# A new order for the first 620 steps of an mLSTM and two-FFN kernel, with other engines for some of its small operations

## The chip, the cores and the metric

One core of one Trainium2 chip runs the whole kernel. Its engines work side by side, each through a list of its own in order: TensorE (PE) multiplies, VectorE (DVE), ScalarE (ACT) and GpSimd (POOL) do the elementwise work, SyncE (SP) issues the transfers. The metric is the device time of one execution in microseconds; lower is better.

## The reference

Three layers follow one another. B = 4, H = 8, S = 768, D = 40.

```python
# 1. gated linear attention, over t for every batch and head
m_new = max(f[t] + m, i[t])
C = exp(f[t] + m - m_new) * C + exp(i[t] - m_new) * outer(v[t], k[t])
n = exp(f[t] + m - m_new) * n + exp(i[t] - m_new) * k[t]
y[t] = sigmoid(o[t]) * (C @ q[t]) / max(abs(n @ q[t]), 1)
# 2. feed-forward layer on x = y, 3072 rows of 320
h = x @ w_in                          # 320 x 2048
x1 = (max(h, 0) + alpha * min(h, 0)) @ w_out   # 2048 x 320
# 3. eight experts; each row goes to the one with the largest x1 @ w_gate
out = prob * sigmoid(x1 @ w_output_gate[e]) * (max(x1 @ w1[e], 0) @ w2[e])
```

w_in and w_out arrive as 64-bit floats, everything else as 32-bit floats.

## The kernel before

**Precision.** Large products are made of two single-precision numbers in TensorE's fast format: a value is split into a high part (a copy by ACT) and a low part (value minus high part, by DVE or POOL). A product is three partial products. Every split is therefore one ACT instruction and one DVE or POOL instruction.

**Tiling.** Attention works on 24 units u of 128 positions, all eight heads at once; unit u is chunk c = u mod 6 of batch u div 6. The first FFN works on eight blocks n of three units (384 columns), each with 16 slices of 128 hidden features, so that there are 128 pairs k = 16 n + i. The experts follow in slots of 128 rows that were sorted by expert; they lie behind all that the change touches.

**Column tiles.** The product of decayed scores and values (att_b) and that of w_out with the gates' weights (gate_w2) are cut into four products with 32 output partitions each, which run in four column groups of TensorE.

**The order.** Attention, weight decoding, FFN and the expert weights' splitting are cut into steps. `ORDER` is a list of short codes; the n-th time a code appears, its step function is called with its n-th argument. Each step appends its instructions to the engines' lists, and the framework adds the waits. There is no other scheduling: an engine runs its own instructions in the order in which `ORDER` named them, and waits where one is not ready.

```python
with tc.manual_schedule():
    for code in ORDER.split():
        fn, args = steps[code]
        a = next(args)
        fn(*a)
```

The list has 1,616 codes. What they mean:

- `li` / `lo` (load_wi, load_wo; SP, L641) bring one of 16 blocks of w_in / w_out into one of three raw tiles, which the experts' pieces (`el`, L1197) share. `di` / `do` (dec_wi, dec_wo) decode one from 64 to 32 bits in three DVE instructions (L658, L660, L662). `si` / `so` (split_wi, split_wo) split it: ACT at L674 / L691, then DVE or POOL at L675 / L692.
- `gw`, `gc`, `gv`, `gs` carry the gate weights into w_out: transposes (PE, L699), a copy (ACT, L705), products in column tiles (PE, L714), and the split of the result (ACT L720, DVE L721).
- `lq`, `lv`, `lg`, `load_g`, `log` load q and k, k and v, grouped q, decay rows (D) and output gates of attention. `load_gates`, `load_sel`, `load_cst`, `load_wg` and `ga`, `gb`, `gm`, `gates_st`, `ge`, `gt`, `gates_d` make the gates' cumulative decays at the start.
- `ae` (att_e) takes the exponential of the decay rows (ACT, four of L754; POOL's mask, L755); `as` (att_s) makes the scores (PE, L764); `am` (att_m) multiplies the two (DVE, L772); `ab` (att_b) multiplies by the values (PE, L863).
- `pt` (prep_kt) scales the keys (DVE or POOL, L732); `ad` (att_d) makes the state's increment (PE, L817); `au` (att_u) masks it (DVE L837, or ACT in three instructions L835); `av` (att_v) adds it to the decayed state (DVE, L852).
- `ah` (att_h) multiplies q by the state (PE, L786); `an` (att_n) scales that (DVE L807, or ACT in eight instructions L805); `aa` (att_a) adds it to the unit's own part (DVE, L873).
- `ay` (att_y) has five parts: three for the divisor (DVE, L882, L884, L886), the scaling (part 3, "att_r": DVE L894, or ACT in eight instructions L892), and the gating (part 4, "att_y": DVE or POOL, L898, with a copy on POOL, L899). `ac` and `ax` transpose the unit (PE, L910) and split it into the block's x (ACT L920, DVE L921 and L922).
- `F` (ffn1) is the first product of a pair k: eight matmuls of 384 columns (PE, L933) into one of two PSUM banks. `f` (ffn_act) is the leaky ReLU (ACT L946, DVE L948); for k under 24 its result goes to SBUF (v), after that back to PSUM (ph). `g` (ffn_split) splits it (ACT L954, DVE or POOL L955). `S` (ffn2) is the second product: nine matmuls of 336 columns (PE, L967, L968, L970).
- `es` (expert_split) and `et` split a piece of an expert's weights (ACT L1205, DVE or POOL L1206) and store it.

Attention's small products take turns in three PSUM banks, which the step that reads a product gives back.

**The engine of a step.** `OTHER` names, for ten kinds of steps, the indices that do not use the usual engine:

```python
def engine(usual, other, name, i):
    return other if i in OTHER.get(name, ()) else usual
```

Usual engine, and the other one: ffn_split DVE, POOL; prep_kt DVE, POOL; att_y POOL, DVE; expert_split POOL, DVE; att_n, att_r, att_u, att_v DVE, ACT; split_wi and split_wo POOL, DVE.

Of the kernel before, what the change touches and what calls it, by code (L numbers as in the profile page):

```python
# [18 lines left out]
B, H, S, D = 4, 8, 768, 40  # L19
# [97 lines left out]
ae lg lg S g S S F f g ad au av pt ah an ay es F f g ab aa F f ay ay ad au av et ae et S g el load_g el F f es ay  # L117
et F f ay ay ac ax S g es ae S g ah an F f S S et es ay ay et g lv el el bp as am F f F f el g es et pt S S ab aa
ac ax g ad au av F f F f g S g ay lq sg es es S ay lv pt F f ay el lq g F f as am S g F f et es ah an ad au av S
log S g bo F f sg et g load_g load_g ay ay el el F f lg S ae ab aa ay ay ay et S F f S g lq lq S g ae ac ax lg el S  # L120
as am lv load_g load_g load_g es et es et ay ay F f pt F f g g ab aa ae ay ac ax F f S g es ay ay ay ay S F f F f
ae as am lq S g g load_g ah an ad au av ac ax ae el F f lv pt el ae g et ab aa ay ay S es es F f et et g load_g ay
F f S g as am ay ay lv S load_g S F f g F f ah an ab aa ay S el el es ad au av lg ay ae g ay el es F f ac ax g
load_g et et ah an ah an lv es et ae bp ay ay S S S ae as am F f g F f load_g bo g ab aa ae load_g ae F f g S lq el
# [1308 lines left out]
```

## Time and profile before

| | us |
|---|---|
| median of 3 runs | 753.1 |
| lowest and highest run | 750.1 to 753.96 |
| the profiled execution, its own time | 749.58 |
| its span, first to last instruction | 747.7 |
| PE busy | 717.1 (96%) |
| DVE busy | 463.0 (62%) |
| ACT busy | 368.0 (49%) |
| POOL busy | 184.4 (25%) |

The profile is one execution. Its own time has 1.9 us beside the span. Busy time is the time in which an engine had an instruction under way; for PE it includes the overlap of pipelined matmuls. The mean granted clock of TensorE over the span was 0.994 of full speed.

### The profile page before, as it was taken

The numbers are of one execution on the slowest core, as the hardware profiler recorded it, in microseconds if no ns is written. First come the engines' busy times: TensorE is split into PE (matmuls) and PEld (weight loads), VectorE is DVE, ScalarE is ACT, GpSimd is POOL, SyncE is SP. The second block draws the span as 40 slices with busy tenths as digits, with TensorE's granted clock in tenths as the row PEclk, the third lists the DMA queues.
The fourth block names the chain that finished last, engine by engine and source line by source line (L and its number), as shares of the span: only waits on it lengthen the run. The fifth ranks groups of instructions, "written<-read, shape, count | busy, mean of one in ns | idle before, by whom it ended". The sixth has DMA issues, their size and how long they took to land.

```text
span 747.7 us, 18074 instructions
## 1 busy us (share of the span) xinstructions
PE 717.1 (96%) x6347; PEld 672.7 (90%) x6347; DVE 463.0 (62%) x1119; ACT 368.0 (49%) x840; POOL 184.4 (25%) x240
## 2 busy tenths in 40 slices
PE   5879899999999999999999999999999999999997
PEld 4668889999999999999999999998989999999996
DVE  6879997868676676677797877766323322232222
ACT  4747687736656655656755445433323332333322
POOL 2444454413213332100000100022222222232223
PEclk9989999999999999999999999999999999999999
DMA  7977679879797958778888779885957636921000
GB/s 253 289 206 239 193 239 324 271 272 306 259 324 245 285 183 279 237 238 293 262 290 293 240 272 320 303 310 197 422 226 299 261 138 236 425 73 40 31 14 22
DMA packets 81526, 179.56 MB, mean 240 GB/s; under 512 B 8620, under 2 KB 39209, under 8 KB 80156
## 3 DMA queue, kind: packets, MB, share of 16 engines
q1 hardware_dynamic: 77980, 169.66, 66.1%
q0 software_dynamic: 3456, 8.71, 3.5%
q8 instruction: 56, 0.92, 0.5%
q14 instruction: 34, 0.28, 0.1%
HBM read 246.29 MB, written 55.59 MB: 404 GB/s over the span
## 4 chain that ended last, share of the span: by engine, by line
PE 70%; DVE 9%; DMA 5%; ACT 2%; issue 2%; SPq 1%; POOL 0%; POOLq 0%; ACTq 0%; DVEq 0%
PE ph L933 18%; PE p L326 12%; PE po L326 12%; PE acc L967 7%; PE acc L968 6%; PE acc L970 6%; DMA ring<-scr 3%; PE p L424 3%; PE ps L764 2%; DVE ph L948 1%; PE pb L786 1%; PE pd L817 1%; PE xt L386 1%; PE pa L863 1%; DMA kv<-in_kv_dram 1%
## 5 line engine op out<-in xcount | busy, mean ns | idle before, releaser
L933 PE MATMUL ph<-ring 128*128 128x384 f32 x1024 | 199.7, 343 | 2.7 <-DVE ring L955 2.7
L933 PEld LDWEIGHTS ph<-ring 128*128 128x128 f32 x1024 | 178.1, 189 | 7.0 <-DVE ring L955 5.3
L967 PE MATMUL acc<-ring 128*128 128x336 f32 x384 | 122.6, 324 | 0.3 <-ACT ring L954 0.3
L968 PE MATMUL acc<-ring 128*128 128x336 f32 x384 | 119.4, 317 | 0.0
L946 ACT ACTIVATE v<-ph 128x384 f32<-128x384 f32 x128 | 62.6, 490 | 94.1 <-PE ph L933 90.1
L446 DVE TENSOR_SCALAR yo<-po,xg 128x320 f32<-128x320 f32 x26 | 14.3, 551 | 138.3 <-PE po L326 138.3
L326 PE MATMUL po<-ring,hh 128*128 (+1 forms) x432 | 95.6, 308 | 0.0
L948 DVE SCALAR_TENSOR_TENSOR ph<-v,al,ph 128x384 f32<-128x384 f32 x104 | 63.8, 618 | 45.6 <-ACT v L946 45.2
L326 PE MATMUL p<-ring,xh 128*128 (+1 forms) x324 | 89.9, 399 | 0.8 <-DMA ring<-scr 0.8
L970 PE MATMUL acc<-ring 128*128 128x336 f32 x384 | 80.1, 316 | 0.0
L326 PEld LDWEIGHTS po<-ring,hh 128*128 128x128 f32 x432 | 73.2, 187 | 2.3 <-ACT hh L426 0.2
L967 PEld LDWEIGHTS acc<-ring 128*128 128x128 f32 x384 | 72.2, 188 | 1.9 <-ACT ring L954 0.7
L955 DVE TENSOR_TENSOR ring<-ph,ring 128x384 fp32r<-128x384 f32 x104 | 57.4, 555 | 24.9 <-ACT ring L954 22.8
L954 ACT ACTIVATE ring<-ph 128x384 fp32r<-128x384 f32 x104 | 50.6, 489 | 44.1 <-DVE ph L948 40.6
L968 PEld LDWEIGHTS acc<-ring 128*128 128x128 f32 x384 | 72.2, 188 | 0.0
L426 ACT ACTIVATE hh<-p 128x512 fp32r<-128x512 f32 x54 | 29.5, 596 | 86.3 <-PE p L424 86.3
L326 PEld LDWEIGHTS p<-ring,xh 128*128 128x128 f32 x324 | 58.8, 188 | 12.4 <-DMA ring<-scr 1.0
L447 POOL DMA_INDIRECT out_dram<-yo,tok x28 | 28.2, 1005 | 161.5 <-DVE yo L446 130.0
L413 ACT ACTIVATE hr<-p 128x512 f32<-128x512 f32 x56 | 33.6, 600 | 68.3 <-PE p L326 64.7
L326 PE MATMUL po<-ring,hl 128*128 (+1 forms) x216 | 66.6, 308 | 0.2 <-DVE hl L428 0.2
L970 PEld LDWEIGHTS acc<-ring 128*128 128x128 f32 x384 | 63.6, 189 | 0.0
L754 ACT ACTIVATE D<-D,EKT 128x128 f32<-128x128 f32 x192 | 60.3, 394 | 1.6 <-DMA D<-gd 1.5
(211 smaller groups left out, 1102.1 us busy)
## 6 DMA issues: line engine op xcount, KB each, us to landing
ring<-scr SPq DMA_DIRECT2D x26, 3072.0 KB
ring<-scr SPq DMA_DIRECT2D x26, 2560.0 KB
ring<-scr SPq DMA_DIRECT2D x33, 512.0 KB
D<-gd SPq DMA_DIRECT2D x48, 256.0 KB
er<-in_ew_dram SPq DMA_DIRECT2D x32, 384.0 KB
scr<-ring SPq DMA_DIRECT2D x32, 384.0 KB
scr<-er SPq DMA_DIRECT2D x32, 384.0 KB
er<-in_ew_dram SPq DMA_DIRECT2D x32, 320.0 KB
```

What stands on the lines that cost most here:

```text
L326: mm = T.matmul(o_, lhsT, r, start=start, stop=stop)
L413: A.activation(hr_half(j, hf), ph, AF.Relu)
L426: A.activation(hh[:, hs], pts[j, hf], AF.Copy)
L754: A.activation(d[:, j], d[:, j], AF.Exp, bias=EKT[:, c, i + j : i + j + 1])
L933: T.matmul(ph[:, :384], wi_[i][lo][:, wc], xTs[n % 2][:, xc], start=(a == 0), stop=(a == len(PASSES) - 1),)
L946: A.activation(v, ph[:, :384], AF.Relu, scale=-1.0)
L948: V.scalar_tensor_tensor(g, v, al1[:, i : i + 1], ph[:, :384], ALU.mult, ALU.add)
L954: A.activation(gh, v, AF.Copy)
L955: engine(V, G, "ffn_split", k).tensor_tensor(gl, v, gh.bitcast(F32), ALU.subtract)
L967: T.matmul(ac, gh[:, sl], hi, start=(i == 0), stop=False)
L968: T.matmul(ac, gh[:, sl], lo, start=False, stop=False)
L970: T.matmul(accs[n][t][:, :NO], gl[:, t * P : (t + 1) * P], hi, start=False, stop=(i == NFC - 1))
```

## The change

Nothing is computed in another way. The first 620 codes of `ORDER` are the same codes in another order; the remaining 996 are the same in the same order. Each kind of step has as many codes ahead of code 621 as it had. In `OTHER`, the sets of indices change:

- ffn_split: twelve of the first 27 pairs were on POOL, nine are. prep_kt: units 0 and 4 go to DVE, unit 2 to POOL. att_y: units 3 and 6 go to POOL, unit 8 to DVE. expert_split: pieces 2, 4 and 5 go to POOL, piece 8 to DVE.
- att_n of units 4 and 8, att_r of unit 7 and att_u of units 0 and 4 go to ACT.
- split_wi and split_wo: as many on DVE as before (five and seven), other blocks.

The diff; of `ORDER`, its first lines on either side (from code 621 on, the lines are only broken in other places):

```diff
@@ -49,35 +49,34 @@
 
 OTHER = {
     "ffn_split": (
-        1, 4, 6, 7, 8, 9, 10, 12, 13, 16, 17, 18,
+        4, 5, 7, 8, 10, 11, 13, 15, 19,
     ),
     "prep_kt": (
-        0, 1, 3, 4, 7, 8, 10, 13, 14, 15, 16,
+        1, 2, 3, 7, 8, 10, 13, 14, 15, 16,
     ),
     "att_y": (
-        3, 4, 5, 6, 11, 13, 16, 17, 18, 19, 20, 21, 22, 23,
+        4, 5, 8, 11, 13, 16, 17, 18, 19, 20, 21, 22, 23,
     ),
     "expert_split": (
-        0, 1, 2, 4, 5, 9, 11, 12, 13, 14, 15, 18, 19, 20, 25, 26, 27, 30, 31, 32, 33, 34, 35, 36, 37, 38,
-        39, 40, 41, 42, 43, 44, 45, 46, 47, 48, 49, 50, 51, 52, 53, 54, 55, 56, 57, 58, 59, 60, 61, 62,
-        63,
+        0, 1, 8, 9, 11, 12, 13, 14, 15, 18, 19, 20, 25, 26, 27, 30, 31, 32, 33, 34, 35, 36, 37, 38, 39,
+        40, 41, 42, 43, 44, 45, 46, 47, 48, 49, 50, 51, 52, 53, 54, 55, 56, 57, 58, 59, 60, 61, 62, 63,
     ),
     "att_n": (
-        3, 5,
+        3, 4, 5, 8,
     ),
     "att_r": (
-        5,
+        5, 7,
     ),
     "att_u": (
-        2, 3, 6,
+        0, 2, 3, 4, 6,
     ),
     "att_v": (
     ),
     "split_wi": (
-        1, 2, 7, 8, 15,
+        0, 4, 6, 7, 11,
     ),
     "split_wo": (
-        0, 1, 6, 7, 9, 11, 13,
+        0, 3, 6, 8, 9, 12, 15,
     ),
 }
 
@@ -95,45 +94,45 @@
 
 
 ORDER = """
-load_gates load_sel ga ah lo do do do lo do do do gb gm load_cst gw load_wg gc an gw gc so li so di ge gv gv gs gt
-lv lo gates_d do do do gw lq gs di pt so ad au gc gt gates_st lv as di li di load_g load_g pt load_g ae ae di di am
-gv av ab aa si li si lo lg gs di log ae do do do ay ay ay ay lg ad sg ay lq load_g load_g lo au lo lv di load_g lq
-gw di ah av an gc gv gs si ac ax as do do ae am do lo do do ah ab load_g do so so an li ae aa log ay ay ae ay ay lo
-lo gw gw gc gc lq as ay do do do am ac di di di so lo ax do ab aa so si do ay ay gw ay ay do do load_g ay gc gv gs
-set_al1 do load_g do gv gs gv gs pt so ac ax li di di so gw ae ae gc gw gc F F di si f li load_g f gv gs log do do
-do di di g so lg lg gv gs el es g lv ad au F F lq di f lq lo av S lo ae pt as am S lq ah si g do do do do do f ad
-an lv pt au gw do li gc av so g F ab f pt ae aa ay gw ay gw gc gc F lo et di di as so li li li do li di S S si do g
-do gw ay ay f so F lo lg li li S lv am g S di di di di di lg load_g gv gv gv f di sg g ah gs gs lo si si an di di
-di di di load_g load_g F f si F ab ad di f ay gc F do gs au av aa S sg si do gv ac li di di do li li ay g di gs f
-load_g g ay S gw so ax ay si F S gc gv ay di av load_g di g do di do ae ay ae as F do gs f am ah ah si F an ac g di
-di di f ax lv ab aa lo si ay so f gw gc g S g ad ay ay ay pt di di F S load_g lv av S S di el di gv di as di si lq
-ay f au lq F ae ae ac do do load_g lg am ab aa si g ae ad an load_cst2 ax log ay F F es f gs do au f ae gw gc
-load_g pt ay ay ay F gv gs as ay g g so f S S S ad et am ah el el lv es f lq ab load_g lq el g pt ac F F sg es an
-aa ay bo f au av ay ax lg S g S f et g ay F F ay et es et g ah ad ay F f g S an au av f ae el f S es el es lg ac lg
-load_g load_g g g ax as et et el ae ae ae am el F f F ah an lq es et es S ab aa ay g as F S S load_g ay ay F lv el
-el S f lq f g S ay ay F F et f g S g am ab ac bp pt lv ad F F f g es et f g f f el S g S S S au av aa load_g el ay
-ay es es ay pt ah an ax lg g ay ay pt et lg ae es F f S et g F f log ad au av g ae et as am ae S bo F f g F f
-load_g ae ab aa ay el lv el S g ay es el F f as am g load_g load_g es et es et F f load_g ac ax lv ah an el el ae
...
+load_gates load_cst lo load_sel ga do gb lo lo do do do load_wg lq gw lv lo gm gates_st do do lv so gc gv ge gs gt
+so gates_d do gw gc do do do so gw do do gc gt li lo gv pt gw so do di di load_g load_g gs di li ad gv gc lg gv
+load_g li ae si ah au di gs as di load_g di gs ae si ae ae do ah am pt do di an an ab aa di di ay so ay lq as si gw
+ay ay log av am lo do sg lg do load_g do ad au av ab aa gc ay ay li lo ac do ay ay ay ae ax ah an so do do gw gc lq
+as di di di load_g ae gw lv am ay load_g ab aa ay li pt si ae gc ac ay ay ay lv ax gv lo lo log ay load_g load_g gs
+do do so load_g gv do li gs lo so gv do ac gw set_al1 do ax F gs di do F el ae gw ae di di f si lq lq lg gc di di f
+ad gc di gv gv g so gs S F do lo ae gs lv do as au do av si F f am ah pt ad es g do do g do so lo do do do F an et
+f f gw gc ab aa load_cst2 li li au av lo so S gw S lg ay ay di ay F gw so load_g gc ay di g gv di di di di g gv li
+gs gs gc si si do do pt sg ay di S do f g S log di di si as F F li li am so di gw ah di di gv li li gc gs f gv S di
+di an ad si lq f di di ab lo lg lg pt lv F au F av li load_g g S g load_g sg load_g ac si f di di aa f g gs si F F
+lv lg ah S S ad ay ax ay di di di di ah ae ay ay as si do do load_g g S ae an do gw f di ay ae di gc g F am si f li
+ac ax lq lq gv gs ab aa F g f ay lo pt S ae di S ae li ay ay load_g ay as lq lo di di ay g S ac ad av am so ab aa
+au f si F di lg g S lq el do av lg load_g load_g di di ax do do au ah f do do do si load_g el gw F an F an gw el f
+ay F ay ay so es gc gv gc gv ay lv as so gs g g f ay S gs ae es S am f ae et et bo F F lv ac el as lq g g S ae F pt
+log f f F el lq g ae am ad ab ab F g ax f f load_g load_g au es et av ah F bp aa ay el ay es et S ay an pt ay aa S
+S g S ad ay g f g es lv lv f ac ax au F F S ae S f et f g ay es ay load_g el av as g g pt am F el ah ay ay sg an ab
+et es es S F S F et el S f lq g el ay ac lg et ad F F f g es et f g f f el S g S S S au av aa load_g el ay ay es es
+ay pt ah an ax lg g ay ay pt et lg ae es F f S et g F f log ad au av g ae et as am ae S bo F f g F f load_g ae ab
...
```

## Rows read from the trace of the kernel before

**Rows 1.** Busy time by stretch: PE, PEld, DVE, ACT, POOL; clock, DMA share.

```profile
46.00:53.00 7.00, 5.90 (x45) 5.42 (x38) 5.58 (x16) 5.26 (x16) 3.97 (x6) 0.52 0.72 179
53.00:118.00 65.00, 60.47 (x828) 55.87 (x827) 60.57 (x138) 47.09 (x134) 28.51 (x33) 1.00 0.75 236
118.00:165.00 47.00, 47.00 (x525) 45.20 (x525) 34.72 (x81) 29.28 (x65) 20.11 (x23) 1.00 0.85 282
```

**Rows 2.** The chain that ended last, 100 to 130 us: start, us, what.

```profile
113.67 0.30 DVE ring L922
...
114.11 0.87 PE pd L817 x6
...
118.11 1.41 PE ph L933 x8
119.52 0.31 PE pwg L714 x24
...
122.52 0.15 PE acc L967
...
123.91 0.15 PE acc L967
...
125.94 0.67 PE pb L786 x6
```

**Rows 3.** Timeline of PE at F(0) with F(1), and at F(29).

```profile
49.49 4.53 PE L933 MATMUL ph<-ring 128*128 128x384 f32 x16
...
164.64 1.66 PE L933 MATMUL ph<-ring 128*128 128x384 f32 x8
```

**Rows 4.** Groups by line, 0 to 165 us: busy, mean ns, idle before.

```profile
L955 DVE TENSOR_TENSOR ring<-v,ring 128x384 fp32r<-128x384 f32 x12 | 10.5, 889 | 1.6 <-ACT ring L954 1.6
...
L692 DVE TENSOR_TENSOR ring<-f_wo,ring 128x320 fp32r<-128x320 f32 x7 | 3.3, 484 | 0.8 <-ACT ring L691 0.8
...
L955 DVE TENSOR_TENSOR ring<-ph,ring 128x384 fp32r<-128x384 f32 x4 | 2.2, 557 | 0.8 <-ACT ring L954 0.7
L837 DVE TENSOR_TENSOR pd<-pd,cst 120x369 f32<-120x369 f32 x4 | 2.2, 540 | 0.0
...
L898 DVE TENSOR_TENSOR y<-y,so 128x320 f32<-128x320 f32 x4 | 1.9, 478 | 0.0
L732 DVE TENSOR_TENSOR kt<-kv,EKT 128x320 f32<-128x320 f32 x3 | 1.6, 533 | 0.5 <-DMA kv<-in_kv_dram 0.5
...
L894 DVE TENSOR_TENSOR y<-pa,dn 128x320 f32<-128x320 f32 x8 | 3.9, 490 | 0.2
L1206 DVE TENSOR_TENSOR er<-er,ring 128x768 fp32r<-128x768 f32 (+1 forms) x6 | 5.5, 910 | 0.2 <-ACT ring L1205 0.2
```

**Rows 5.** Timeline of DVE and SP, 45 to 51 us: a raw tile's turn.

```profile
45.69 0.48 DVE L662 SCALAR_TENSOR_TENSOR f_wo<-r_wo,f_wo 128x320 int32<-128x320 int32 x1
...
46.20 2.33 SPq L641 DMA_DIRECT2D r_wi<-in_wi_dram  x2
...
50.04 0.36 DVE L658 TENSOR_SCALAR f_wi<-r_wi 128x384 int32<-128x384 int32 x1 [0.28 <-POOL ring L692]
```

**Rows 6.** Timeline of ACT: a scaling in eight instructions, a mask in three.

```profile
104.34 1.59 ACT L892 ACTIVATE y<-pa,dn 128x40 f32<-128x40 f32 x8 [0.32 <-DVE dn L886]
...
115.02 0.88 ACT L835 ACTIVATE state<-pd,cst 120x123 f32<-120x123 f32 x3 [0.65 <-PE pd L817]
```

**Rows 7.** Timeline, 147 to 153 us: POOL's expert splits, a DVE split.

```profile
148.57 3.37 POOL L1206 TENSOR_TENSOR er<-er,ring 128x640 fp32r<-128x640 f32 x2 [1.75 <-ACT ring L1205]
...
150.45 1.89 DVE L955 TENSOR_TENSOR ring<-v,ring 128x384 fp32r<-128x384 f32 x1 [0.77 <-ACT ring L954]
```

**Rows 8.** Timeline of DVE: the first w_out split, and f(1).

```profile
10.89 0.89 DVE L692 TENSOR_TENSOR ring<-f_wo,ring 128x320 fp32r<-128x320 f32 x2 [0.80 <-ACT ring L691]
...
54.58 0.61 DVE L948 SCALAR_TENSOR_TENSOR v<-v,al,ph 128x384 f32<-128x384 f32 x1 [1.01 <-ACT v L946]
```

More of the change, by code (lines that the diff above doesn't have):

```diff
@@ L113 @@
-load_g load_g g g ax as et et el ae ae ae am el F f F ah an lq es et es S ab aa ay g as F S S load_g ay ay F lv el
-el S f lq f g S ay ay F F et f g S g am ab ac bp pt lv ad F F f g es et f g f f el S g S S S au av aa load_g el ay
-ay es es ay pt ah an ax lg g ay ay pt et lg ae es F f S et g F f log ad au av g ae et as am ae S bo F f g F f
-load_g ae ab aa ay el lv el S g ay es el F f as am g load_g load_g es et es et F f load_g ac ax lv ah an el el ae
-ae lg lg S g S S F f g ad au av pt ah an ay es F f g ab aa F f ay ay ad au av et ae et S g el load_g el F f es ay
@@ L118 @@
[L118 to L122, printed above, removed]
@@ L123 @@
-F f S g as am ay ay lv S load_g S F f g F f ah an ab aa ay S el el es ad au av lg ay ae g ay el es F f ac ax g
-load_g et et ah an ah an lv es et ae bp ay ay S S S ae as am F f g F f load_g bo g ab aa ae load_g ae F f g S lq el
-S ac ax F f g load_g pt S pt F f lg load_g ae as am el es lq F f S g S el g es et F f et g ay ay el F f ae ab aa g
-ay ay ay ay F f load_g lv F f S lq S ad au av g g es et es et el ad au av pt ae ac ax S F f g S el el as am F f F f
-log g S S g es et lg bp es et F f F f g S g S load_g el S es et F f g F f log el el ae ay ay g S S bo es F f lg F f
@@ L128 @@
-ah an g S es as am sg ay ay et et g F f g lq ab aa ay S F f g el el S es load_g load_g sg F f F f S g ay ad au av g
-es ae ac ax et S lv et ay ay ay pt F f es F f ah an ab aa ay ay lg el ae g S g es ay lv ad au av pt S F f F f el g
-ac ax ah an et es et S load_g ay ay ae g el el F f es S g lg S ad au av F f et es F f lq et et g el el ac ax bp S g
-S S F f g F f S es es g F f g et S S bo as am el es F f F f g et lv pt el el et as am ab aa ay es et ay ay load_g S
-S g lg el load_g first_set ah an lq ab aa el ay ay ay F f g F f S g ad au av ae es F f F f lv es g S g ac ax S S ae
@@ L133 @@
-ay ay ay ay as am et et es et ac ax F f g F f S el el el bp g F f ah an ab aa g es es ay ay ay ay ay F f F f S S S
-g g et es et el S et el F f g F f el S es es g F f et et ac ax g S S es et F f g ld el el F f g S F f g S bo ld es
-F f F f S g g route_a S F f F f S g el g S bh bh bh et ld ld ld ad au av bh ld ld bh bh bh F f ld S ld es S ld ld g
-es F f g bh bh S bh bh F f g F f S et bh ld g ld S bp F f F f ld bh g bh bh bh bh S S bh route_first bh bh bh g F f
+load_gates load_cst lo load_sel ga do gb lo lo do do do load_wg lq gw lv lo gm gates_st do do lv so gc gv ge gs gt
@@ new lines @@
+et es es S F S F et el S f lq g el ay ac lg et ad F F f g es et f g f f el S g S S S au av aa load_g el ay ay es es
+ay pt ah an ax lg g ay ay pt et lg ae es F f S et g F f log ad au av g ae et as am ae S bo F f g F f load_g ae ab
+aa ay el lv el S g ay es el F f as am g load_g load_g es et es et F f load_g ac ax lv ah an el el ae ae lg lg S g S
+S F f g ad au av pt ah an ay es F f g ab aa F f ay ay ad au av et ae et S g el load_g el F f es ay et F f ay ay ac
+ax S g es ae S g ah an F f S S et es ay ay et g lv el el bp as am F f F f el g es et pt S S ab aa ac ax g ad au av
@@ new lines @@
+F f F f g S g ay lq sg es es S ay lv pt F f ay el lq g F f as am S g F f et es ah an ad au av S log S g bo F f sg
+et g load_g load_g ay ay el el F f lg S ae ab aa ay ay ay et S F f S g lq lq S g ae ac ax lg el S as am lv load_g
+load_g load_g es et es et ay ay F f pt F f g g ab aa ae ay ac ax F f S g es ay ay ay ay S F f F f ae as am lq S g g
+load_g ah an ad au av ac ax ae el F f lv pt el ae g et ab aa ay ay S es es F f et et g load_g ay F f S g as am ay
+ay lv S load_g S F f g F f ah an ab aa ay S el el es ad au av lg ay ae g ay el es F f ac ax g load_g et et ah an ah
@@ new lines @@
+an lv es et ae bp ay ay S S S ae as am F f g F f load_g bo g ab aa ae load_g ae F f g S lq el S ac ax F f g load_g
+pt S pt F f lg load_g ae as am el es lq F f S g S el g es et F f et g ay ay el F f ae ab aa g ay ay ay ay F f
+load_g lv F f S lq S ad au av g g es et es et el ad au av pt ae ac ax S F f g S el el as am F f F f log g S S g es
+et lg bp es et F f F f g S g S load_g el S es et F f g F f log el el ae ay ay g S S bo es F f lg F f ah an g S es
+as am sg ay ay et et g F f g lq ab aa ay S F f g el el S es load_g load_g sg F f F f S g ay ad au av g es ae ac ax
@@ new lines @@
+et S lv et ay ay ay pt F f es F f ah an ab aa ay ay lg el ae g S g es ay lv ad au av pt S F f F f el g ac ax ah an
+et es et S load_g ay ay ae g el el F f es S g lg S ad au av F f et es F f lq et et g el el ac ax bp S g S S F f g F
+f S es es g F f g et S S bo as am el es F f F f g et lv pt el el et as am ab aa ay es et ay ay load_g S S g lg el
+load_g first_set ah an lq ab aa el ay ay ay F f g F f S g ad au av ae es F f F f lv es g S g ac ax S S ae ay ay ay
+ay as am et et es et ac ax F f g F f S el el el bp g F f ah an ab aa g es es ay ay ay ay ay F f F f S S S g g et es
@@ L137 @@
+et el S et el F f g F f el S es es g F f et et ac ax g S S es et F f g ld el el F f g S F f g S bo ld es F f F f S
+g g route_a S F f F f S g el g S bh bh bh et ld ld ld ad au av bh ld ld bh bh bh F f ld S ld es S ld ld g es F f g
+bh bh S bh bh F f g F f S et bh ld g ld S bp F f F f ld bh g bh bh bh bh S S bh route_first bh bh bh g F f
 route_first2 first_rows S g F f g ld S F f F f S ld ld g S ld ld ld pt ld ld g first_x first_x S bo bp et first_1
```

## Prediction

> **What bounds the kernel now.** I read the busy table by stretch first, then the chain that ended last, then the timeline around three products, then the groups by line. In the stretch from 53 to 118 us VectorE (DVE) works 60.57 of 65 us, with its gaps mostly short, while TensorE (PE) shows 60.47 busy but only 55.87 of weight loads; from 118 to 165 us PE is busy for 47.00 of 47 and DVE for 34.72 [rows 1]. The chain says the same: until 113.97 us it runs over DVE (the last piece is the x split at 113.67), and from 114.11 on it runs over PE alone [rows 2]. So the first 620 steps have two halves: one in which DVE's decoding of the 32 weight blocks decides, and one in which PE only works off what is left. After them stands the same list in both kernels, so what the change can give is the earlier start of its first product, F(29), now at 164.64 us [rows 3]. F(17), at 118.11 us in the chain [rows 2], is about where DVE hands over to PE: a time for F(29) is the time at which DVE has done what stands ahead of F(17), plus the PE work between the two.
>
> How much is there to get at most? Per product PE needs 1.41 us for a first-layer product F (eight matmuls), 1.39 for a second-layer product S (from 122.52 to 123.91), 0.67 for the state product ah and 0.31 for the gate product gv [rows 2]. The 29 F and 26 S ahead of F(29) are 77 us of the 164.64 it takes. The rest is attention, gates and waiting, so a better order has tens of us in principle; but DVE is nearly full up to 118 us, and only the less work it has ahead of F(17) counts.
>
> **The change part by part.** All steps of the first 620 are the same in number; they stand in another order, and some go to another engine. I count what stands ahead of F(17) in either list.
>
> *DVE ahead of F(17).* Two masks att_u (0.540 each) are gone to ScalarE (ACT); one kt product comes (0.533); one gated output (0.478), one att_y division (0.490), one expert split (0.910) and one w_out split (0.484) stand later or elsewhere; two FFN splits come from POOL [rows 4]. Three instructions on 8 or 16 columns that also stand later are left out. A FFN split on DVE shows two prices: 0.557 with its input in PSUM, 0.889 on the mean with its input v in SBUF, up to 1.89 [rows 4, 7]. With 0.557 the sum is -1.080 + 0.533 - 0.478 - 0.490 - 0.910 - 0.484 + 1.114 = -1.8 us; with 0.889 it is -1.1. The 1.89 lies under POOL's expert split, which ran from 148.57 to 151.94 [rows 7]. I take 0.557: what is over it is waiting for POOL, and POOL has less ahead of F(17) in the new list (two FFN splits fewer there, two kt products and one mask fewer, one gated output more).
> The Trainium skill ("SBUF — State Buffer", Who interferes with whom) says that a DVE instruction with two SBUF inputs is blocked for as long as a GpSimd instruction that reads SBUF holds the shared port. The trace agrees with it by the 1.89 against 0.557. By that rule the FFN splits that move to DVE are better priced at the mean of 0.889, and the whole sum below would come out 0.7 smaller.
>
> *PE behind F(17).* One S and one ah more, and one gv less, stand ahead of F(17): 1.39 + 0.67 - 0.31 = 1.75 us less PE work between F(17) and F(29) [rows 2], provided that PE has room for it earlier. It has: 65 - 55.87 us of the DVE-bound stretch had no weight load [rows 1].
>
> *Waits that go.* The first w_out split waits 0.80 for ACT, because two copies of transposed weights stand ahead of it on ACT [rows 8]; in the new list it is ACT's first work. The second leaky-ReLU step waits 1.01 for ACT [rows 8]; now a w_in split and two decode steps stand between f(0) and f(1), over 1.4 us of DVE work, which covers it. Together -1.8, if ACT is in time.
>
> *Waits that come.* The raw weight tile has three buffers, and a load waits until one has been decoded. In the trace the last decode of a block ended at 46.17, the next load was issued at 46.20, and that block's first decode ran at 50.04 after 0.28 idle: 3.8 us for a turn [rows 5]. In the new list lo(4) takes the buffer that do(2,2) frees, and its decode comes after three decodes (0.48 each), a kt product and a split, 2.5 us [rows 4, 5]. So 1.4 us are bare; 0 if DVE has waited elsewhere by then, 3.8 if the transfer is as slow as the turn and nothing covers it. In unit 5 the output's scaling stays on ACT (8 instructions, 1.59 us [rows 6]), but its gating on DVE now comes after two decodes only, about 1.0 us: 0.6 us bare; 0 to 1.6 for the same reasons.
>
> *Work moved to ACT.* att_n for units 4 and 8 and att_r for unit 7 are eight ACT instructions each, 1.59 us as a row [rows 6]; att_u for units 0 and 4 is three, 0.88 [rows 6]. Together 3 x 1.59 + 2 x 0.88 = 6.5 us. I cost them at nothing: ACT is busy 47.09 of 65 and 29.28 of 47 us in the two halves [rows 1]. Without that cover they hold ACT's copies v and gh, which DVE's f and g wait for; those f free the two PSUM banks of F.
>
> *Expert splits.* Two more splits net (2, 4 and 5 to POOL, 8 back) leave DVE, after F(17), where DVE has 47 - 34.72 us to spare [rows 1]: nothing.
>
> *The sum.* -1.8 (DVE) - 1.75 (PE) - 1.8 (waits gone) + 1.4 + 0.6 (waits new) = -3.3 us on F(29), which passes undiminished to the end if the rest stays PE-bound. The profiled execution took 749.58, so 746.3; it is faster than the runs' median of 753.1, and on that the forecast is 749.8 us.
>
> **The rivals.**
> *All waits covered (faster).* If neither new wait shows, the gain is 5.3 us: 747.8 on the runs' scale. For it speaks that DVE's waits are cheap where it is late already; the granted clock adds to it: from 46 to 53 us it was 0.52, close to the lower level of 1.2 GHz, so F(0) and F(1) took 4.53 us together, where 16 matmuls take 2.80 at full clock by the later rows (2 x 1.41) [rows 1, 2, 3]. If PE's steadier work ahead of F(0) raises the clock earlier, 1.7 us more: 746.1. Against it: PE had nothing to do in a large part of that stretch in both orders.
> *Given back later (no change).* F(29) comes 3.3 us earlier, but the expert weights, whose loads and splits stand at the same places, or PSUM banks make the rest wait: 753.1. For it: 583 us follow. Against it: PE is the chain from 114 us on [rows 2], and it had no idle time from 118 to 165 [rows 1].
> *ACT in the way (slower).* ACT takes its list in order. If the 6.5 us in bursts of 1.59 stand ahead of copies that DVE and PE need at once, ACT is late, and the 1.8 us of waits for ACT stay too: -1.8 - 1.75 + 2.0 + 6.5 = +5.0, so 758.1. Place: units 4, 7 and 8, around F(7) to F(24). It cancels the gain once 3.3 us of the 6.5 are uncovered, and shows as slower from about 7 us (with the waits that stay). Against it: at 47.09 of 65 us ACT idles 27% of the time, and its bursts of unit 3 and 5 in the old kernel left DVE 93% busy.
>
> **How the numbers follow.** About 0.5%, 3.8 us, is what a measurement of this kernel can tell from no change. Forecast (gain 2 to 4.5): 0.42, of which a third lies beyond 3.8. All waits covered: 0.27. Given back: 0.18. ACT in the way: 0.13, of which 0.11 beyond 3.8 and the rest within. Faster: 0.27 + 0.14 = 0.41; slower 0.11; within 0.48. The range reaches down to 745 (the first rival with the clock, and a little of DVE's other short gaps) and up to 755.5 (half of the third rival), the forecast's own is 748.5 to 751.
>
> **What would show it.** F(29) should start between 160 and 162.5 us, with F(17) at about 116, and the chain should change from DVE to PE there or earlier. DVE should be idle some 1.4 us ahead of the fifth w_out decode and under 1 us ahead of unit 5's gating; the first w_out split should not wait. From F(29) to the end the time should be 583 us as before. The forecast is wrong if F(29) is early by other than 2 to 5 us, if the stretch behind it is longer by what was gained, or if DVE or PE wait for ACT behind the eight-fold scalings.

## Result and the profile after

The changed kernel took 745.45 us (median of 6 runs, 743.45 to 748.16) beside 754.08 of the kernel before on the same chip: a ratio of 0.9893 [0.9864, 0.9923]. Run again later beside 25 runs of the kernel before (median 751.89) it took 746.69 (10 runs), a ratio of 0.9941 [0.9922, 0.9959]. The brackets are 95% intervals; a ratio comes from the runs themselves and is not quite the quotient of the medians. So the gain is between 4 and 9 us; the two profiled executions, 749.58 and 743.45, differ by 6.1. Forecast were 3.3.

The busy table by stretch of the kernel after (columns as in [rows 1]), first the stretches of [rows 1], then cut at the start of F(17) and of F(29):

```profile
46.00:53.00 7.00, 6.97 (x81) 6.08 (x80) 6.30 (x14) 6.17 (x20) 2.41 (x3) 0.81 0.60 172
53.00:118.00 65.00, 64.00 (x831) 59.36 (x830) 58.44 (x138) 48.36 (x142) 28.32 (x32) 1.00 0.80 238
118.00:165.00 47.00, 46.78 (x491) 45.49 (x490) 33.00 (x80) 31.69 (x82) 18.64 (x24) 1.00 0.93 303
0.00:113.91 113.91, 97.93 (x1311) 87.30 (x1311) 98.06 (x241) 77.11 (x218) 47.62 (x62) 0.96 0.82 242
113.91:159.59 45.68, 45.46 (x535) 43.70 (x533) 33.35 (x82) 32.13 (x86) 19.96 (x24) 1.00 0.93 297
159.59:741.70 582.11, 573.42 (x4509) 542.22 (x4507) 325.51 (x793) 263.77 (x567) 116.33 (x154) 1.00 0.68 238
```

The same three cuts in the kernel before:

```profile
0.00:117.86 117.86, 96.77 (x1319) 85.73 (x1320) 101.86 (x245) 75.48 (x210) 47.61 (x63) 0.97 0.77 239
117.86:164.64 46.78, 46.78 (x526) 44.98 (x524) 34.46 (x81) 29.42 (x65) 20.11 (x23) 1.00 0.86 283
164.64:747.70 583.06, 573.54 (x4509) 542.03 (x4507) 326.65 (x795) 263.10 (x566) 116.64 (x154) 1.00 0.68 237
```

The cuts are starts of products in PE's timeline (F(17) of the kernel before stands there at 117.86, 0.25 us ahead of the chain's row that the prediction took). Of the kernel after (F(0), F(17) and F(29)):

```profile
46.72 4.00 PE L932 MATMUL ph<-ring 128*128 128x384 f32 x16
...
113.91 1.66 PE L932 MATMUL ph<-ring 128*128 128x384 f32 x8
...
159.59 2.70 PE L932 MATMUL ph<-ring 128*128 128x384 f32 x14
```

What the reader is to see: F(17) starts 3.95 us earlier, the stretch from F(17) to F(29) is 1.10 shorter, and the tail 0.95 shorter. That is all of the 6.0 us between the two spans. Up to F(17) DVE is busy 98.06 instead of 101.86 us, and idle 113.91 - 98.06 = 15.85 instead of 16.00. So, as a sum, the whole lead at F(17) is less DVE time at work. Its idle time, where I had put half of the argument, is the same. A sum is not yet a cause: busy time that falls can turn into waiting, and in two of the experiments it does. Behind F(17), PE is full in both kernels. Why the tail is 0.95 shorter is not shown; in a second profile of the changed kernel (after_again) it took 582.67, 0.4 less than before.

Where DVE's 3.80 us went, in its groups by line. Kernel after, until F(17) (columns as in [rows 4]; line numbers are one lower than before):

```profile
L661 DVE SCALAR_TENSOR_TENSOR f_wi<-r_wi,f_wi 128x384 int32<-128x384 int32 x16 | 10.9, 684 | 0.4
...
L659 DVE SCALAR_TENSOR_TENSOR f_wo<-r_wo,f_wo 128x320 int32<-128x320 int32 x16 | 8.9, 554 | 0.4
...
L954 DVE TENSOR_TENSOR ring<-v,ring 128x384 fp32r<-128x384 f32 x7 | 4.2, 599 | 0.0
L691 DVE TENSOR_TENSOR ring<-f_wo,ring 128x320 fp32r<-128x320 f32 x6 | 3.5, 580 | 0.0
...
L674 DVE TENSOR_TENSOR ring<-f_wi,ring 128x384 fp32r<-128x384 f32 x5 | 2.8, 576 | 0.7 <-ACT ring L673 0.6
...
L731 DVE TENSOR_TENSOR kt<-kv,EKT 128x320 f32<-128x320 f32 x3 | 2.1, 706 | 0.0
```

Kernel before, until F(17):

```profile
L662 DVE SCALAR_TENSOR_TENSOR f_wi<-r_wi,f_wi 128x384 int32<-128x384 int32 x16 | 12.1, 758 | 0.3
...
L660 DVE SCALAR_TENSOR_TENSOR f_wo<-r_wo,f_wo 128x320 int32<-128x320 int32 x16 | 9.3, 583 | 0.4
...
L955 DVE TENSOR_TENSOR ring<-v,ring 128x384 fp32r<-128x384 f32 x5 | 3.7, 737 | 0.0
L675 DVE TENSOR_TENSOR ring<-f_wi,ring 128x384 fp32r<-128x384 f32 x5 | 3.4, 701 | 0.5 <-ACT ring L674 0.5
...
L692 DVE TENSOR_TENSOR ring<-f_wo,ring 128x320 fp32r<-128x320 f32 x7 | 3.3, 484 | 0.8 <-ACT ring L691 0.8
...
L732 DVE TENSOR_TENSOR kt<-kv,EKT 128x320 f32<-128x320 f32 x2 | 1.1, 568 | 0.5 <-DMA kv<-in_kv_dram 0.5
```

The same number of instructions costs another time: sixteen third decode steps of w_in fall from 758 to 684 ns each (-1.2 us), five w_in splits from 701 to 576 (-0.6).

### The profile page after: what moved, and what is told of

It reads as the page before. It is cut to its first block, busy times and chain, and to the rows that moved or that the text cites. A ratio compares the mean times of both kernels' runs of the same rounds, so it can differ in the third digit from the quotient of the medians.

```text
span 741.7 us, 18086 instructions
## 1 busy us (share of the span) xinstructions
PE 716.8 (97%) x6347; PEld 673.2 (91%) x6347; DVE 456.9 (62%) x1115; ACT 373.0 (50%) x870; POOL 183.9 (25%) x239
```

## Experiments

Each ratio is to the kernel before on the same chip. F(17), F(29) are starts, busy and idle are DVE's until F(17), all of the profiled execution, in us.

| kernel | median | ratio, 95% | F(17) | F(29) | busy | idle |
|---|---|---|---|---|---|---|
| before | 751.6 to 754.1 | 1 | 117.86 | 164.64 | 101.9 | 16.0 |
| changed | 745.45 | 0.9893 [0.9864, 0.9923] | 113.91 | 159.59 | 98.1 | 15.9 |
| after_again | 746.69 | 0.9941 [0.9922, 0.9959] | 114.44 | 160.03 | 98.2 | 16.3 |
| order_main | 753.83 | 1.0021 [1.0004, 1.0038] | 121.27 | 169.67 | 101.8 | 19.5 |
| engines_only | 769.22 | 1.0231 [1.0201, 1.026] | 133.15 | 185.12 | 104.4 | 28.8 |
| new_start | 762.28 | 1.0144 [1.0118, 1.017] | 126.09 | 177.90 | 100.5 | 25.5 |
| old_start | 754.79 | 1.0048 [1.0026, 1.0071] | 122.94 | 168.38 | 100.3 | 22.7 |
| act_back | 745.96 | 0.9934 [0.9913, 0.9956] | 115.01 | 161.27 | 99.4 | 15.6 |
| ffn_back | 747.89 | 0.9963 [0.9942, 0.9984] | 116.72 | 162.03 | 100.0 | 16.7 |
| wo_back | 748.67 | 0.9964 [0.9942, 0.9986] | 117.44 | 162.99 | 98.9 | 18.6 |
| kt_back | 745.98 | 0.9915 [0.9887, 0.9944] | 114.15 | 160.73 | 96.6 | 17.6 |
| ayes_back | 746.13 | 0.9928 [0.9903, 0.9954] | 114.88 | 161.70 | 98.9 | 16.0 |
| order_three | 748.57 | 0.9960 [0.9943, 0.9977] | 116.61 | 163.13 | 100.0 | 16.6 |
| pool_memset | 751.10 | 0.9999 [0.9978, 1.0019] | 120.47 | 167.08 | 99.5 | 21.0 |

**Order or engines?** order_main has the new order with the engine sets of before, the w_in splits excepted.

```diff
     "ffn_split": (
-        4, 5, 7, 8, 10, 11, 13, 15, 19,
+        1, 4, 6, 7, 8, 9, 10, 12, 13, 16, 17, 18,
...
     "att_u": (
-        0, 2, 3, 4, 6,
+        2, 3, 6,
...
     "split_wo": (
-        0, 3, 6, 8, 9, 12, 15,
+        0, 1, 6, 7, 9, 11, 13,
```

> The new order with the old engines, but for the w_in splits, which stay as in the changed kernel (five on DVE in both). Theory W (what stands ahead of F(17) on DVE decides, counted with its waiting for POOL, and then the PE work left behind F(17)): in this list DVE has 1.4 us less ahead of F(17) than before by the rows' durations, and PE has 1.75 us less behind it, so F(29) leads that of before by some 3 us and the time is 3 to 5 us under before's (ratio 0.993 to 0.996). Rival E (the moves to other engines bring it): within 1 us of before. Rival O (the order alone brings it, the engines are incidental): the whole gain, ratio 0.989.

engines_only has the new engine sets and the first 620 codes of before.

```diff
     "ffn_split": (
-        1, 4, 6, 7, 8, 9, 10, 12, 13, 16, 17, 18,
+        4, 5, 7, 8, 10, 11, 13, 15, 19,
...
     "att_u": (
-        2, 3, 6,
+        0, 2, 3, 4, 6,
```

> The old order with the new sets of engines. Theory W: DVE has 1.0 us less ahead of F(17), PE nothing less behind it: 0 to 2 us under before (ratio 0.997 to 1.000). Rival E: the larger part of the gain, 4 us or more (ratio 0.994 or less). Rival O: within 1 us, or slower, since ACT has 6.5 us more in an order that was not made for it.

The order by itself gains nothing (1.0021), the engines by themselves lose 17 us. No theory stands: order_main missed the range of W and lies nearest to that of E, which engines_only refutes; O had allowed for a slower engines_only, but falls with order_main. In engines_only the first product of scores and decays in DVE (L771) is 2.7 us later than before (21.84 against 19.14). Its timeline of DVE, ACT and POOL up to there:

```profile
15.39 1.15 DVE L731 TENSOR_TENSOR kt<-kv,EKT 128x320 f32<-128x320 f32 x1
...
18.39 0.87 ACT L834 ACTIVATE state<-pd,cst 120x123 f32<-120x123 f32 x3 [3.23 <-PE pd L816]
...
19.81 2.45 ACT L753 ACTIVATE D<-D,EKT 128x128 f32<-128x128 f32 x8
21.17 0.63 POOL L754 TENSOR_SCALAR_AFFINE_SELECT D<-D 128x512 f32<-128x512 f32 x1 [1.96 <-ACT D L753]
...
21.84 0.69 DVE L771 TENSOR_TENSOR D<-ps,D 128x512 f32<-128x512 f32 x1 [3.37 <-POOL D L754]
```

Unit 0's mask, new on ACT, waited 3.23 us for its PE product. The product was late because unit 0's kt product, new on DVE, began there at 15.39; before, POOL had begun it at 13.49. The decay tiles D queued behind the mask on ACT came later with it, POOL waited for them, and DVE waited 3.37 for POOL. So two moves together do it: one makes the product late, the other lets ACT wait for it. The second is the prediction's rival "ACT in the way", with its price in one place: 3.4 us. Until F(17), DVE's listed waits that end on ACT come to 12.7 us, against 5.9 before; the rest of the 12.8 us more idle time was not followed up. In the new order the first of these decay tiles stands ahead of unit 0's mask on ACT, at 17.47 us.

**Half of the order.** Both kernels have the new engine sets; new_start has the new list up to F(0) and then the steps left over in the old order, old_start the reverse.

```diff
 ORDER = """
-load_gates load_sel ga ah lo do do do lo do do do gb gm load_cst gw load_wg gc an gw gc so li so di ge gv gv gs gt
+load_gates load_cst lo load_sel ga do gb lo lo do do do load_wg lq gw lv lo gm gates_st do do lv so gc gv ge gs gt
...
```

> The new engines; the new list up to F(0) (184 codes), then the remaining codes as the old list has them. Theory W: the count ahead of F(17) is that of the old list with new engines, 1.0 us less than before, nothing less for PE: 0 to 3 us under before. Theory C (the start decides: F(0) comes 2.8 us earlier and TensorE's clock is granted in full 4 us earlier): F(29) leads by 3 us or more, ratio 0.994 or less.

> The new engines; the old list up to F(0) (191 codes), then the remaining codes as the new list has them. Theory W: F(17) has the new list's count ahead of it, so most of the gain, 3 to 5 us in the profile, ratio 0.990 to 0.994. Theory C: within 2 us of before, since F(0) comes as late as before.

Both mixtures lose, 10 and 2.5 us, and neither theory foresaw it: W wanted both faster than before, and C's earlier F(0) did not come (49.53 us in new_start, 54.90 in old_start, 49.49 before). So old_start has lost its time by F(0), new_start loses it behind F(0). DVE's idle time follows the fit of list and sets: 16 us where they belong together, 19.5 to 29 in the four mixtures; its busy time is between that of the two kernels in these two (100 us), and above both in engines_only. The time from F(29) to the end was 582 to 586 us in every kernel of the table, so all of them are decided ahead of F(29).

**The changed kernel again.**

> The changed kernel once more, with a profile of its own. In the profiles so far the first product F(0) starts at 46.72 us in the changed kernel, but at 49.5 in the kernel with the new list up to F(0) and the old one behind it (new_start), though the list up to F(0) and the engine sets are the same. Theory 'what follows reaches forward' (engines run ahead of F(0) into the steps behind it, so that a later list changes what DVE, POOL and the queues do before F(0)): F(0) starts at 46.7 within 0.5 us again, F(17) at 113.9 and F(29) at 159.6 within 1 us, DVE busy 98 us until F(17). Rival 'one lucky execution': F(0) moves towards 49 and F(29) to 161 to 162. Either way the ratio to the kernel before is 0.986 to 0.993.

F(17), F(29) and busy came back within 0.6 us; F(0) stood at 46.91. The question in the expectation rested on a slip: in new_start ten more steps stand ahead of F(0), so its 49.5 needs no other cause. What it leaves is how far an execution varies: 743.5 to 748.7 over ten runs, so that, by the width of the intervals, single sets below 1.5 us or so can't be told from nothing by their medians.

**Which engine set?** The changed kernel with one kind of step put back on the engines of before.

```diff
     "att_n": (
-        3, 4, 5, 8,
+        3, 5,
...
     "att_r": (
-        5, 7,
+        5,
...
     "att_u": (
-        0, 2, 3, 4, 6,
+        2, 3, 6,
```

> The changed kernel's order, with the steps att_n, att_r and att_u of units 0, 4, 7 and 8 put back on the engines that the kernel before has for them (the 6.5 us of ScalarE work go; DVE gets 1.6 us more ahead of F(17), POOL the rest). Theory 'order and engines are matched' (the list was laid out with these steps on ScalarE, and a step that runs on another engine pushes everything queued behind it there): idle time of DVE ahead of F(17) rises from 15.8 to 18 us or more, F(29) moves from 159.6 to 163 to 165, ratio to the kernel before 0.995 to 1.002. Rival 'the terms add up' (only DVE's work counts): F(29) at 161 to 161.5, idle unchanged, ratio 0.990 to 0.993. Rival 'ACT in the way': the kernel gets faster than the changed one, ratio 0.980 to 0.986.

```diff
     "ffn_split": (
-        4, 5, 7, 8, 10, 11, 13, 15, 19,
+        1, 4, 6, 7, 8, 9, 10, 12, 13, 16, 17, 18,
```

> The changed kernel's order and engines, only the twenty pairs' FFN splits on DVE or POOL as in the kernel before. Ahead of F(17) DVE has two such splits fewer (1.1 us at 0.557 each) and POOL two more. Theory 'shared port' (part of the gain is that DVE's decoding and splitting, which read two SBUF inputs, are held up less because POOL splits less): DVE's busy time until F(17) does not fall by 1.1 us but stays at 98 us or rises, since its other instructions take longer under POOL's splits; ratio to the kernel before 0.989 to 0.994. Rival 'instruction counts alone': DVE busy 97 us until F(17), F(29) at 158.5, ratio 0.986 to 0.989. Rival 'order and engines are matched': DVE idle ahead of F(17) rises by 2 us or more, ratio 0.992 to 0.998.

```diff
     "split_wo": (
-        0, 3, 6, 8, 9, 12, 15,
+        0, 1, 6, 7, 9, 11, 13,
```

> The changed kernel's order and engines, only the sixteen w_out splits on DVE or POOL as in the kernel before (both sets have seven on DVE; split 1 goes to DVE, split 3 to POOL, and others later). What has to be found is 8 us: the new order with nearly all old engines (order_main) took 753.8 against 746 for the changed kernel, of which the att steps (act_back, nothing in time) and the FFN splits (ffn_back, 1 to 3 us) are tried. Theory 'one split in the wrong place at the start' (in order_main DVE waited 1.05 us in the second w_out split and was 2.4 us later in the first w_in decode, because split 1 stood on DVE just ahead of decodes): the first w_in decode, at 17 to 18 us in the changed kernel, comes 1.5 to 2.5 us later, F(17) at 116.5 or later, ratio to the kernel before 0.995 to 0.999. Rival 'counts' (DVE has 0.5 us more ahead of F(17) by the groups' means): F(17) at 114.4, ratio 0.991 to 0.994. Rival 'the sum of many': the loss appears only where several sets go back together; ratio 0.993 or less here and in the two runs beside it.

```diff
     "prep_kt": (
-        1, 2, 3, 7, 8, 10, 13, 14, 15, 16,
+        0, 1, 3, 4, 7, 8, 10, 13, 14, 15, 16,
```

> The changed kernel's order and engines, only the kt products on DVE or POOL as in the kernel before (units 0 and 4 go to POOL, unit 2 to DVE). DVE has 0.5 us less ahead of F(17) and POOL 0.7 us more. Theory 'counts': F(17) 0.5 us earlier than 113.9 to 114.4, ratio 0.990 to 0.993. Theory 'engines must match the order' (POOL is now late with a kt product on which unit 0's attention or a w_in split behind it hangs, and DVE waits for POOL): DVE idle ahead of F(17) up by 1.5 us or more, ratio 0.995 to 1.000.

```diff
     "att_y": (
-        4, 5, 8, 11, 13, 16, 17, 18, 19, 20, 21, 22, 23,
+        3, 4, 5, 6, 11, 13, 16, 17, 18, 19, 20, 21, 22, 23,
...
     "expert_split": (
-        0, 1, 8, 9, 11, 12, 13, 14, 15, 18, 19, 20, 25, 26, 27, 30, 31, 32, 33, 34, 35, 36, 37, 38, 39,
+        0, 1, 2, 4, 5, 9, 11, 12, 13, 14, 15, 18, 19, 20, 25, 26, 27, 30, 31, 32, 33, 34, 35, 36, 37, 38,
```

> The changed kernel's order and engines, only the gated outputs (att_y) and the expert splits on DVE or POOL as in the kernel before: units 3 and 6 to DVE, unit 8 to POOL; expert splits 2, 4 and 5 to DVE, 8 to POOL. The prediction priced the expert splits at nothing. DVE has 2.2 us more ahead of F(29) by the groups' means, 0.5 of it ahead of F(17). Theory 'counts, covered behind F(17)': F(17) 0.5 us later than 113.9 to 114.4, F(29) no more than that, ratio 0.991 to 0.994. Rival 'the uncovered output of unit 3' (in order_main DVE waited 1.00 us for the scaling on ScalarE ahead of unit 3's gating, which then stood on DVE): F(17) at 115.5 to 116.5, ratio 0.994 to 0.997. Rival 'expert splits on DVE hold products': F(29) later by 1.5 us or more than F(17) is.

The 6.5 us of work on ACT, the kt products and the outputs with the expert splits change nothing that the medians show; in the profiles F(29) is 0.7 to 2.1 us later than in the two of the changed kernel. In ayes_back 1.1 to 1.2 us of this lie behind F(17), where PE waited 1.0 us for DVE, so the expert splits that the prediction put at nothing are not quite free there. "Matched", the theory of act_back, fell: DVE has 1.3 us more to do there, and no more idle time. Of its three theories "the terms add up" is nearest. In kt_back DVE is busy 1.5 us less and idle 1.3 to 1.7 us more: F(17) stays where it was, so the work saved went into waiting.

The FFN splits and the w_out splits cost 1 to 3 us each by the medians; their intervals overlap that of after_again, so the loss rests on the later F(29) as well. ffn_back is the telling one: two splits fewer on DVE, and yet DVE is busy 1.9 us longer, as "shared port" had it (its ratio missed that theory's range). wo_back lost its 2 to 3 us mostly not at the start, as I had expected. The first w_in decode is 1.2 to 1.4 us later (18.47 us), and the second w_out split does wait,

```profile
12.19 0.49 DVE L691 TENSOR_TENSOR ring<-f_wo,ring 128x320 fp32r<-128x320 f32 x1 [1.06 <-ACT ring L690]
```

but F(0) stands at 47.15 us in that kernel, against 46.72 and 46.91 with the new set. Most of the loss comes in small pieces between F(0) and F(17): of the 2.3 to 2.7 us more idle time, 1.5 to 2.3 lie there. TensorE's granted clock from 46 to 53 us was 0.50 in this execution, against 0.81 and 0.64; what that cost was not separated.

**The order with three new sets only.** All that cost nothing alone is put back together; the sets for w_in, w_out and FFN splits stay new.

```diff
     "prep_kt": (
-        1, 2, 3, 7, 8, 10, 13, 14, 15, 16,
+        0, 1, 3, 4, 7, 8, 10, 13, 14, 15, 16,
...
     "att_n": (
-        3, 4, 5, 8,
+        3, 5,
```

> The new order with three new engine sets only (w_in splits, w_out splits, FFN splits); kt products, gated outputs, expert splits and all att steps stand on the engines of the kernel before. Each of these put back by itself cost nothing in time (act_back 745.96, kt_back 745.98, ayes_back 746.13 against 746.69 and 745.45 for the changed kernel), the w_out splits put back cost 2 us (wo_back 748.67), the FFN splits 1 to 2 (ffn_back 747.89), while order_main, which has all of them back, took 753.83. Theory 'two sets carry it' (the splits of w_out and of the FFN must match the order, the other sets are free): ratio to the kernel before 0.989 to 0.995, F(29) at 160 to 162.5, DVE idle ahead of F(17) 15.5 to 17.5 us. Rival 'small losses add up when slack is used up' (each set alone is covered by slack that the others use too): ratio 0.995 to 1.001, F(29) at 164 or later. By the groups' means DVE has 1.6 us more ahead of F(17) than in the changed kernel.

The median is 748.57, F(29) lies between the two theories' ranges, and the ratio, 0.9960, in that of the rival. Idle is as "two sets carry it" wants (16.6), but busy is 1.9 us higher than in the changed kernel, close to the 1.6 that the groups' means gave for it. So the sets that looked free cost some DVE time together; it is not the sum of what they did alone (+1.3, +0.8 and -1.5). order_main, with the old w_out and FFN sets besides, is another 5 us slower, so these two sets carry the larger part.

**Does POOL lengthen DVE's decodes?** In the kernel before, each FFN split on POOL became two POOL memsets of the same tile, which read nothing; twelve pairs' low parts are left out of the result.

```diff
-            engine(V, G, "ffn_split", k).tensor_tensor(gl, v, gh.bitcast(F32), ALU.subtract)
+            if engine(V, G, "ffn_split", k) is G:
+                for _ in range(2):
+                    G.memset(gl.bitcast(I32), 0)
+            else:
+                V.tensor_tensor(gl, v, gh.bitcast(F32), ALU.subtract)
```

> The kernel before, except that each FFN split that POOL does is replaced by two POOL memsets of the same tile, which read nothing; the low parts of these twelve pairs' hidden values are left out of the result (zeros stand in their place). Order, engines and waits are as in the kernel before; POOL is as long at work with them as the two memsets take. Theory 'shared port': what holds DVE is POOL's reading of SBUF, so DVE's instructions with two SBUF inputs that lie under these POOL instructions show their short duration: DVE's busy time until F(17) falls by 2 to 3 us from 101.9, and F(17) starts 1.5 to 3 us earlier than 117.9. Rival 'any POOL access to SBUF holds DVE, writing too': busy within 0.7 us of 101.9 and F(17) within 1 us of 117.9. Rival 'the length of DVE's instructions has nothing to do with POOL': the same numbers, with long decodes that do not lie over POOL's memsets.

In the timeline of the kernel before, two third decode steps lie under a POOL split:

```profile
58.30 0.95 DVE L1206 TENSOR_TENSOR er<-er,ring 128x768 fp32r<-128x768 f32 x1
58.56 1.56 POOL L955 TENSOR_TENSOR ring<-v,ring 128x384 fp32r<-128x384 f32 x1 [4.91 <-ACT ring L954]
59.17 1.36 DVE L662 SCALAR_TENSOR_TENSOR f_wi<-r_wi,f_wi 128x384 int32<-128x384 int32 x1
...
89.70 1.13 POOL L955 TENSOR_TENSOR ring<-v,ring 128x384 fp32r<-128x384 f32 x1 [1.35 <-ACT ring L954]
...
89.96 1.29 DVE L662 SCALAR_TENSOR_TENSOR f_wi<-r_wi,f_wi 128x384 int32<-128x384 int32 x1
```

The same two steps in pool_memset, and between them two POOL memsets with a two-input decode step that starts under the second:

```profile
61.70 0.55 DVE L662 SCALAR_TENSOR_TENSOR f_wi<-r_wi,f_wi 128x384 int32<-128x384 int32 x1
...
78.38 1.11 POOL L957 MEMSET ring<- 128x384 int32 x2
...
79.16 0.56 DVE L660 SCALAR_TENSOR_TENSOR f_wi<-r_wi,f_wi 128x384 int32<-128x384 int32 x1
...
93.25 0.55 DVE L662 SCALAR_TENSOR_TENSOR f_wi<-r_wi,f_wi 128x384 int32<-128x384 int32 x1
```

1.36 and 1.29 became 0.55 and 0.55 (1.55 of the 2.05 us by which the group of sixteen fell), the group's mean went from 758 to 630 ns, and DVE's busy time until F(17) from 101.9 to 99.5, as "shared port" had it. The Trainium skill ("SBUF — State Buffer", Who interferes with whom) says so: a DVE instruction with two SBUF inputs contends with a GpSimd one that reads SBUF, "not with one that only writes it", and who issued first goes first. The trace agrees on both: 0.56 over a memset, and at 58.56 it is POOL's split that came second to DVE's and took 1.56, where POOL's nine such splits have a median of 1.02.

But the time did not fall (0.9999), and F(17) came 2.6 us later, not earlier: that half of the expectation missed. Idle rose to 21.0. The largest piece of it, in the profiled execution, on ACT and then on DVE:

```profile
59.95 0.84 ACT L1209 ACTIVATE ring<-er 128x768 fp32r<-128x768 f32 x1 [3.33 <-DMA er<-in_ew_dram]
```

```profile
60.83 0.96 DVE L1210 TENSOR_TENSOR er<-er,ring 128x768 fp32r<-128x768 f32 x1 [2.97 <-ACT ring L1209]
```

So DVE time that is taken away reaches the end only if what DVE does next has arrived. The tile's load was issued at 52.28 us there and at 51.96 before, where ACT split it without a wait at 57.22. So the transfer itself took over 2 us longer, though the edit changes neither it nor its place in the list. Whether it did in the timed runs stays open; that fewer holds on DVE make this kernel faster is therefore not shown by pool_memset.

## Why the prediction was near, and where it failed

- **The frame held.** The gain is the lead of F(29), and it passes on: 583.06 us behind it before, 582.11 after. "Given back later" did not happen. F(29) came 5.05 us earlier instead of 3.3, just outside the 2 to 5 that I had set. The measured 745.45 is outside the forecast's own 748.5 to 751 and just inside the low end of the range, 745. That end was drawn for other reasons (no waits, and an earlier clock), so it is luck that the range holds.
- **The step that failed is the term "DVE ahead of F(17)": -1.8 forecast, -3.8 measured.** By the groups until F(17), the pieces that I did sum came to only -0.9. The masks (-1.08), the gated output (-0.46) and the expert split (-0.96) were right. The kt product cost 0.98, not 0.53 (3 x 706 against 2 x 568). The w_out splits gave nothing (6 x 580 against 7 x 484 is +0.09, not -0.48), the att_y division, which is the scaling of L894, nothing until F(17) (five on either side). The FFN splits cost 0.5 instead of 1.1 (7 x 599 against 5 x 737). What I had priced at zero, because its number doesn't change, gave -2.3: the 96 decode steps -1.6, the five w_in splits -0.6. The remaining -0.6 are the short instructions that I left out and small differences.
- **Why the unchanged groups got cheaper.** POOL's busy time until F(17) is the same (47.61 and 47.62), so it is not that POOL does less, as I had argued; it is which DVE instructions fall under its reads. pool_memset shows that mechanism for the FFN splits, ffn_back shows its sign in the new order, and the timelines show it for every group, the dearer ones (kt, w_out splits) too. Until F(17), 24 of DVE's decode steps, splits and kt products in the kernel before run more than 0.06 us over the undisturbed ones of their kind, 9.3 us in all; in the kernel after 18 do, 7.5 us (after_again: 18 and 7.8). Each of them overlaps a POOL instruction that reads SBUF. The leaky ReLU, whose other input is in PSUM, takes 0.61 us with POOL at work or not. So of the 3.8 us some 1.8 are fewer holds, and some 2.0 are fewer instructions at their undisturbed price, which is near the -1.8 of the forecast, by luck in its pieces. A kt product and a w_out split in the kernel after, both 0.48 alone:

```profile
14.70 1.17 POOL L691 TENSOR_TENSOR ring<-f_wo,ring 128x320 fp32r<-128x320 f32 x1 [1.24 <-ACT ring L690]
15.06 1.15 DVE L731 TENSOR_TENSOR kt<-kv,EKT 128x320 f32<-128x320 f32 x1
...
75.60 0.99 POOL L674 TENSOR_TENSOR ring<-f_wi,ring 128x384 fp32r<-128x384 f32 x1
75.88 1.07 DVE L691 TENSOR_TENSOR ring<-f_wo,ring 128x320 fp32r<-128x320 f32 x1
```

  They overlap POOL by 0.81 and 0.71 us and are 0.67 and 0.59 longer: as an estimate from these rows, whoever comes second is longer by the overlap less 0.1 us or so. order_main holds DVE for 10.1 us, engines_only for 12.5, ffn_back for 10.4, so the fewer holds need the order and the engines together. I had seen the 1.89 under POOL's split [rows 7], and used it to price one group instead of all that read two SBUF tiles.
- **The waits were right in sum, by luck, and half wrong one by one.** Forecast were -1.8 + 2.0 = +0.2 us; DVE's idle time changed by -0.15. The first w_out split and the second leaky ReLU wait no more, as forecast; the raw tile's turn and unit 5's gating show 0.20 and 0.37 instead of 1.4 and 0.6. DVE's timeline after:

```profile
10.79 0.48 DVE L691 TENSOR_TENSOR ring<-f_wo,ring 128x320 fp32r<-128x320 f32 x1
...
16.82 0.33 DVE L657 TENSOR_SCALAR f_wo<-r_wo 128x320 int32<-128x320 int32 x1 [0.20 <-DMA r_wo<-in_wo_dram]
...
102.67 0.49 DVE L897 TENSOR_TENSOR y<-y,so 128x320 f32<-128x320 f32 x1 [0.37 <-ACT y L891]
```

  Others took their place, which the list alone did not tell: 1.2 us for a raw tile of w_in, 1.0 for a transpose on PE, 0.9 for constants of the gates. So "All waits covered" came nearest in time, but not by its mechanism.
- **PE behind F(17): -1.75 forecast, -1.10 measured** (46.78 to 45.68), with PE busy 45.46 of it, 1.32 less: the mechanism held, the size was 0.65 too large.
- **The clock** from 46 to 53 us was 0.81 instead of 0.52, and F(0) with F(1) took 4.00 instead of 4.53 us. PE was busy 6.97 of these 7 us instead of 5.90. F(17) does not need it: in after_again the same kernel had 0.64, F(0) with F(1) took 5.01 us, longer than before, and F(17) still came at 114.44.
- **"ACT in the way" did not happen here**, and act_back shows that the 6.5 us cost nothing that the medians show. engines_only shows that the rival is real: with the old order DVE's waits that end on ACT are 6.8 us longer than before, in a kernel that is 17 us slower.
- **The runs' scale.** Of the gain in medians (8.6 and 5.2 us), the 6.0 in the spans have a place, though the tail's 0.95 has no cause; the rest I put down to how far runs and sessions differ, which is not shown.

## What to carry to other kernels

Where one engine's reads hold another engine up, price every instruction of the bounding engine that can fall under them, the unchanged ones too: here the groups with equal numbers gave 2.3 of 3.8 us. An order written out by hand and the choice of engines are one object: either half of this change by itself gains nothing or costs 17 us, so a moved step has to be judged by what is queued behind it on its new engine. And a shorter busy time on the bounding engine counts only when its inputs are there earlier too.

## What the runs showed of the hardware

DVE's one-input decode shift is held as well. In the timeline of the kernel after:

```profile
33.28 0.86 POOL L691 TENSOR_TENSOR ring<-f_wo,ring 128x320 fp32r<-128x320 f32 x1
33.30 1.02 DVE L657 TENSOR_SCALAR f_wo<-r_wo 128x320 int32<-128x320 int32 x1
```

It took 1.02 us, against 0.33 at 16.82 above. I had counted only instructions with two SBUF inputs as exposed to POOL. By the Trainium skill (same section) a tensor_scalar can contend when it runs in a two-port mode. No row names the mode, but pool_memset agrees: there the shift is held by memsets too, which only write, and holds them. First the memsets' durations (ns, min/median/max), then two places in the timeline:

```profile
L957 POOL MEMSET ring<- x20: 412/419/630, 53.9 to 125.8; 128x384 int32 x20
```

```profile
78.78 0.35 DVE L658 TENSOR_SCALAR f_wi<-r_wi 128x384 int32<-128x384 int32 x1
78.86 0.63 POOL L957 MEMSET ring<- 128x384 int32 x1
...
95.70 0.89 POOL L957 MEMSET ring<- 128x384 int32 x2
96.20 0.60 DVE L658 TENSOR_SCALAR f_wi<-r_wi 128x384 int32<-128x384 int32 x1
```

The memset at 78.86 began behind a shift and took 0.63 us; the shift at 96.20 began behind the second memset and took 0.60 instead of 0.35. The three memsets over 0.43 us are those that began under a shift. The two-input step at 79.16, over a memset too, kept its 0.56.
